# Sketched attention and a SwiGLU block on one core: nine more units with products of parts, and another order of the down products

## The chip, the cores and the metric

The kernel runs on one core of one Trainium2 chip. The metric is the device time in microseconds (us), as the median of several runs. Engines are named as in the profile: PE is TensorE (PEld its weight loads), DVE is VectorE, ACT is ScalarE, POOL is GpSimd, SP issues the DMAs.

## The reference

```python
# attention: batch 4, heads 4, sequence 1088, head_dim 32, sketches of r = 8
def phi(x):
    a = np.einsum('rd,bhsd->bhsr', S1, x)
    b = np.einsum('rd,bhsd->bhsr', S2, x)
    return np.einsum('bhsi,bhsj->bhsij', a, b).reshape(*x.shape[:-1], r * r)
q_p, k_p = (phi(q), phi(k))
kv = np.einsum('bhsf,bhsd->bhfd', k_p, v)
z = np.sum(k_p, axis=2)
num = np.einsum('bhsf,bhfd->bhsd', q_p, kv)
den = np.einsum('bhsf,bhf->bhs', q_p, z)[..., None] + 1e-06
# x: (4 * 1088, 128), the attention's output with the heads side by side
g = x @ w_gate                          # w_gate, w_val: 128 x 1536
silu = g * (1.0 / (1.0 + np.exp(-g)))
val = x @ w_val
return (silu * val @ w_out).astype(np.float32)   # w_out: 1536 x 128
```

The inputs of the SwiGLU block come as 64-bit floats and are narrowed on the chip.

## The kernel before

**Tiling.** The 4352 tokens stand as columns of `xT` (128 x 4352). They are cut into blocks: the first batch's 1088 tokens into blocks 0, 1 and 2 with 384, 384 and 320 columns, the other 3264 into six blocks of 480 and one of 384 (`HEAD` is the first of these, `line` lists them). The 1536 hidden channels are 12 chunks of 128. A *unit* (i, j) is the gate and the value product of block i with chunk j, the Silu on ACT, and on DVE the product of both into a hidden slot. A *down product* (`down`, L1082) multiplies one hidden slot by its chunk of `w_out` and adds it up in the bank of its block.

**Two kinds of units.** A plain unit (`unit`, L1034) is one fp32 matmul for the gate and one for the value; the trace shows two records for each of them. A unit *of parts* splits weight and tokens into a high and a low part and their difference, all in fp32r: `start_unit` issues two matmuls with the differences (L997) and an ACT copy of the two sums (L1000), `finish_unit` adds four more matmuls (L1010, L1011), then the Silu (L1013) and the DVE product (L1018). `cut_weights` (L871) makes the parts of a weight chunk (three chunks of 128 columns at a time) in four steps: ACT high part, a subtraction, ACT low part, a last step for the difference, where the second and fourth are on POOL or DVE. `cut_tokens` (L881, L884, L889) does so for a block's tokens. Before the change, units of the first batch are plain and all units of the `line` are of parts.

**Order.** Everything is emitted in an order written by hand; each engine works through its own queue in that order. The first batch's units after the opening ones follow `seq`, 30 units with index z from 0 to 29: z 12 to 20 are chunks 6 to 8 of blocks 0, 1, 2, and z 21 to 29 are chunks 9 to 11 of blocks 0, 1, 2. The narrowing of the weights (`narrow`, via `part`) is threaded between the first 22 of them. From z = 17 on each unit is followed by one down product and by one step of `attentions()`, the generator that prepares the attention of the next batches: `turn_keys` and `turn_queries` (DVE transposes), key products (L354, PE), four feature products (L377, DVE), `feature_sums` (L547, POOL), key values and value sums (L388, L717, PE), `fold` (L601 to L608, DVE), query sketches (L342, PE) with their copies (L590, ACT), `query_step` (L745 to L762: the denominators and three pairs of a feature product and a transpose into `phT`, all DVE), and `numerators` (L780, PE) with copies into `xT` (L797, ACT and DVE). The step that ends with the numerators yields "first"; block `HEAD` can be cut after it. When `seq` is done, a loop issues the down products that are left, three at a time, each time with a step of the attention. The last two follow `start_unit` of the first unit of the `line`. Then come the 84 units of the `line`.

**Banks.** PSUM has eight banks here. `bank` hands out single ones in turn (`g0`, `g1`, `g2` and up to z = 16 `acc`), `pair` the pair used longest ago of (0,1), (4,5), (6,7) that is not held, `wide("a")` and `wide("b")` are the pairs (4,5) and (6,7). `let_go` ends a hold.

**Rooms.** `room` has ten slots of 384 columns; the six opening units keep their Silu in slots 0 to 5 until `catch_up` (L1058, POOL) multiplies it in. Tiles with one tag share a number of buffers (`bufs`), and a new one waits for the last reader of the oldest.

## Time and profile before

| | |
|---|---|
| median of 3 runs | 278.8 us (278.59 to 278.91) |
| the profiled execution | 278.89 us, span 277.2 us |
| busy: PE, DVE, ACT, POOL | 271.4, 203.7, 184.5, 98.9 us |
| plain gate and value products (L1034) | 28.7 and 28.0 us busy, 72 records each |
| matmuls of units of parts | L997, L1010, L1011: 84 records for each of the six |
| copies of sums (L1000, ACT) | 84, 78.5 us |
| clock granted to TensorE | full |

The span runs from the first to the last instruction; the profiled execution's own time holds 1.7 us around it. Matmuls are pipelined, so a record's duration overlaps the next one: the distance from start to start is what a matmul costs TensorE. In a row of the groups stand the line, the engine, the operation, output and inputs by name, the count, then busy time and mean duration, then the idle time before them and who ended it. In a timeline stand the start, the time covered by the merged instructions, the engine, the line, the names and the count.

### The profile page before, as it was taken

How to read it: one execution, taken by the hardware profiler on the slowest of the kernel's cores; microseconds unless marked ns; L12 is line 12 of the kernel's file. 1: busy time of each engine (PE TensorE's matmuls, PEld its weight loads, DVE VectorE, ACT ScalarE, POOL GpSimd, SP SyncE). 2: the span in 40 equal slices, each digit the busy share in tenths (PEclk: the TensorE clock that was granted, in tenths of full speed). 3: DMA queues.
4: the chain of work that ended last, by engine and by line, in shares of the span. 5: the costliest groups of instructions: out<-in, count | busy, mean ns of one | idle time of the engine just before them, and what ended most of it. 6: DMA issues, size and time to landing. Idle time of an engine off the chain costs nothing.

```text
span 277.2 us, 5670 instructions
## 1 busy us (share of the span) xinstructions
PE 271.4 (98%) x2169; PEld 198.3 (72%) x2169; DVE 203.7 (74%) x355; ACT 184.5 (67%) x330; POOL 98.9 (36%) x110
## 2 busy tenths in 40 slices
PE   8899999999999999999999999999999999999995
PEld 7645565666766787777577777867887888788994
DVE  3997987977688873887545766967877995987431
ACT  3468665565421586667479898769879878886860
POOL 3313422179820440060034353435425553542000
PEclk9999999999999999999999999999999999999999
DMA  6573195221151123000200020000100200010011
GB/s 192 168 220 79 54 277 185 74 89 57 39 114 28 26 85 94 2 1 0 38 13 4 0 39 0 0 2 10 27 0 2 36 0 1 9 29 0 10 29 28
DMA packets 26139, 14.30 MB, mean 52 GB/s; under 512 B 19840, under 2 KB 24192, under 8 KB 26112
## 3 DMA queue, kind: packets, MB, share of 16 engines
q1 hardware_dynamic: 25456, 13.84, 19.4%
q8 instruction: 17, 0.28, 0.4%
q10 hardware_dynamic: 656, 0.10, 0.2%
q14 instruction: 10, 0.08, 0.1%
HBM read 11.41 MB, written 2.23 MB: 49 GB/s over the span
## 4 chain that ended last, share of the span: by engine, by line
PE 94%; DVE 2%; DMA 2%; ACT 1%; issue 0%; SPq 0%
PE PS L1082 22%; PE PS L1034 16%; PE PS L1010 13%; PE PS L997 13%; PE PS L1011 13%; PE PS L1074 2%; PE PS L1077 2%; PE PS L1076 2%; PE PS L354 2%; PE PS L780 2%; PE PS L342 2%; PE PS L388 2%; DMA kld<-in_k_dram 2%; PE PS L1110 1%; PE PS L497 1%; PE PS L445 1%
## 5 line engine op out<-in xcount | busy, mean ns | idle before, releaser
L1000 ACT ACTIVATE PS<-PS 128x960 f32<-128x960 f32 (+1 forms) x84 | 78.5, 935 | 32.0 <-PE PS L997 31.2
L1018 DVE SCALAR_TENSOR_TENSOR hbuf<-PS,sg 128x480 f32<-128x480 f32 (+1 forms) x84 | 53.7, 640 | 43.6 <-ACT sg L1013 40.8
L1013 ACT ACTIVATE sg<-PS 128x480 f32<-128x480 f32 (+1 forms) x84 | 46.7, 556 | 2.0 <-PE PS L1011 1.2
L997 PE MATMUL PS<-xd,gphq 128*128 128x480 f32 (+1 forms) x84 | 47.3, 564 | 0.0
L1082 PE MATMUL PS<-hbuf,wo 128*128 128x480 f32 (+3 forms) x118 | 45.9, 492 | 0.0
L1010 PE MATMUL PS<-x,graw 128*128 128x480 f32 (+1 forms) x84 | 32.1, 382 | 0.0
L1011 PE MATMUL PS<-x,wb 128*128 128x480 f32 (+1 forms) x84 | 31.6, 376 | 0.0
L997 PE MATMUL PS<-xd,wd 128*128 128x480 f32 (+1 forms) x84 | 31.4, 374 | 0.0
L1010 PE MATMUL PS<-x,w 128*128 128x480 f32 (+1 forms) x84 | 31.4, 374 | 0.0
L1011 PE MATMUL PS<-x,graw 128*128 128x480 f32 (+1 forms) x84 | 31.3, 373 | 0.0
L1034 PE MATMUL PS<-xT,wg 128*128 128x384 f32 (+1 forms) x72 | 28.7, 480 | 0.0
L1034 PE MATMUL PS<-xT,wv 128*128 128x384 f32 (+1 forms) x72 | 28.0, 470 | 0.2 <-DVE wv L286 0.2
L1082 PEld LDWEIGHTS PS<-hbuf,wo 128*128 128x128 f32 x118 | 22.1, 189 | 7.4 <-issue 0.9
L1038 ACT ACTIVATE sg<-PS 128x384 f32<-128x384 f32 (+1 forms) x30 | 13.8, 465 | 18.8 <-PE PS L1034 17.2
L997 PEld LDWEIGHTS PS<-xd,gphq 128*128 128x128 f32 x84 | 15.8, 188 | 10.0 <-ACT PS L1000 6.4
L997 PEld LDWEIGHTS PS<-xd,wd 128*128 128x128 f32 x84 | 15.8, 189 | 9.9 <-issue 6.7
L884 POOL TENSOR_TENSOR x<-xT,x 128x480 fp32r<-128x480 f32 (+1 forms) x6 | 7.2, 1195 | 37.6 <-ACT x L881 37.6
L1034 PEld LDWEIGHTS PS<-xT,wv 128*128 128x128 f32 x72 | 13.4, 190 | 8.9 <-DVE hbuf L1049 0.9
L1034 PEld LDWEIGHTS PS<-xT,wg 128*128 128x128 f32 x72 | 12.9, 189 | 9.3 <-issue 1.2
L1010 PEld LDWEIGHTS PS<-x,graw 128*128 128x128 f32 x84 | 15.7, 187 | 3.5 <-ACT PS L1000 0.8
L1082 PE MATMUL PS<-hbuf,scaled 128*128 128x480 f32 x36 | 17.4, 565 | 0.0
L1010 PEld LDWEIGHTS PS<-x,w 128*128 128x128 f32 x84 | 15.8, 188 | 2.2
(184 smaller groups left out, 494.5 us busy)
## 6 DMA issues: line engine op xcount, KB each, us to landing
kld<-in_k_dram SPq DMA_DIRECT2D x4, 544.0 KB, 4.4
vld<-in_v_dram SPq DMA_DIRECT2D x12, 144.0 KB, 4.7
qld<-in_q_dram SPq DMA_DIRECT2D x3, 544.0 KB, 4.2
raw<-in_moe_w_out_dram SPq DMA_DIRECT2D x4, 384.0 KB, 4.0
raw<-in_moe_w_gate_dram SPq DMA_DIRECT2D x3, 384.0 KB, 3.6
raw<-in_moe_w_val_dram SPq DMA_DIRECT2D x3, 384.0 KB, 3.7
out_dram<-o SPq DMA_DIRECT2D x16, 60.0 KB, 2.0
vld<-in_v_dram SPq DMA_DIRECT2D x4, 112.0 KB, 4.3
```

The source lines that it names most:

```text
L342: nc.tensor.matmul(ps[32 * a : 32 * a + 32, 96 * (c - c0) : 96 * (c - c0) + 96], qT[:, 4 * c + a, :], s123[:, a : a + H, :, :].rearrange(" ...
L354: nc.tensor.matmul(ps[32 * a : 32 * a + 64, 64 * (c - c0) : 64 * (c - c0) + 64], kT[:, c, a : a + 2, :].rearrange("p a t -> p (a t)"), s12 ...
L884: engine.tensor_tensor(out=x0[:, 0:n], in0=x, in1=whole(x1[:, 0:n]), op=ALU.subtract)
L997: nc.tensor.matmul(ps[:, k], w_parts[id(w), j // 3][2][:, j % 3, :], xd, start=True, stop=True)
L1000: nc.scalar.activation(ps, ps, AF.Copy, scale=-1.0 / WHOLE)
L1010: nc.tensor.matmul(ps[:, k], w1, x1, start=False, stop=False, skip_group_check=True)
L1011: nc.tensor.matmul(ps[:, k], wb, x0, start=False, stop=True, skip_group_check=True)
L1013: nc.scalar.activation(sg, ps[:, 0], AF.Silu, scale=WHOLE)
L1018: nc.vector.scalar_tensor_tensor(out=hj[:, 0:n], in0=ps[:, 1], scalar=WHOLE, in1=sg, op0=ALU.mult, op1=ALU.mult)
L1034: nc.tensor.matmul(o[:, 0:n], w[:, j, :], xT[:, t0 : t0 + n], start=True, stop=True)
L1038: nc.scalar.activation(sg[:, 0:n], g[:, 0:n], AF.Silu)
L1082: nc.tensor.matmul(acc[i][:, 0:n], w, hidden[i, j][:, 0:n], **sides)
```

## The change

The units z = 21 to 29 become units of parts, started one ahead. For this the parts of the weight chunks must be there earlier: chunk 3 (channels 9 to 11) of both weights is split at z = 11 to 18, in its own rooms (`home`), with DVE for the second and fourth step. The tokens of blocks 0, 1, 2 are split at z = 18, 21, 24. The other three chunks are split later, much as before. The down products come in another order (blocks 0 and 1 with chunks 0 to 8, then chunks 9 to 11 of both, then block 2), and two of them follow units 17, 18, 21, 22 and 23, so that 18 instead of 13 are issued within the list. `catch_up` moves from z = 24 to 26 to z = 18 to 20. In the attention, pairs are taken by `pair`, the sums of features are issued one by one between the feature products, the second key products with their copies come ahead of the value sums, and one more step is taken at z = 25. The `exp` and `man` tiles have 5 and 4 buffers instead of 6 each.

```diff
+    narrow_bufs = dict(exp=5, man=4)
...
-            stage.tile(shape, I32, tag=n + tag, name=n, bufs=6) for n in ("exp", "man")
+            stage.tile(shape, I32, tag=n + tag, name=n, bufs=narrow_bufs[n]) for n in ("exp", "man")
...
-            lambda: add(s[:, 0:2, :], rows[:, 0:2, :], rows[:, 4:6, :]),
-            lambda: add(s[:, 2:4, :], rows[:, 2:4, :], rows[:, 6:8, :]),
-            lambda: add(s[:, 0:2, :], s[:, 0:2, :], s[:, 2:4, :]),
+            lambda: add(s, rows[:, 0:2, :], rows[:, 2:4, :]),
+            lambda: add(s, s, rows[:, 4:6, :]),
+            lambda: add(s, s, rows[:, 6:8, :]),
...
-        hold("a")
-        kp = wide("a")
+        kp = pair("keys")
...
+            if n == 0:
+                zs, sums = feature_sums(phk)
+            else:
+                sums.pop(0)()
             if n == 3:
-                release("a")
+                let_go("keys")
             if n % 3 != 1:
                 yield
-        zs, sums = feature_sums(phk)
-        for f in sums:
-            f()
+        sums.pop(0)()
         yield from turn_keys(2)
-        kvz = wide("a")
+        kvz = pair("values")
         key_values(kvz[:, 0, 0:F], phk, 0, NC)
+        kab, copies = sketched(pair(), key_products, 2, "kab2")
+        run_copies(copies, 2)
         value_sums(kvz[:, 0, :], zs)
-        kab, kcopies = sketched(wide("b"), key_products, 2, "kab2")
         fold(kvz[:, 0, :])
         spread = spread_out(1, kvz[:, 0, :])
-        hold("a", "b")
+        let_go("values")
         yield
-        qab, copies = sketched(wide("a"), query_sketches, 3, "qab")
+        qab, copies = sketched(pair(), query_sketches, 3, "qab")
         run_copies(copies, 2)
         yield
-        run_copies(kcopies, 2)
-        release("a", "b")
...
+    def home(w, c):
+        if w is wg:
+            if c == 3:
+                return [big("phq", k) for k in range(3)]
+            return [big("raw", k) if k < 8 else big("phq", 3) for k in range(3 * c, 3 * c + 3)]
+        if c == 3:
+            t = const.tile([P, 3, 3, P], F32R, name="v3")
+            return [t[:, k] for k in range(3)]
+        return [
+            stage.tile([P, 3, P], F32R, tag=tag, name=name, bufs=narrow_bufs[tag])[:]
+            for tag, name in (("exp", "w1"), ("man", "wb"), (("exp", "man")[c % 2], "wd"))
+        ]
...
-            acc[i] = bank("g1" if i == 1 else "g2" if i in line[2::2] else "acc")
+            acc[i] = bank("g2" if i == 1 or i in line[2::2] else "acc")
...
-    order = [(i, j) for i in range(3) for j in range(NCH)]
+    order = [(i, j) for i in (0, 1) for j in range(9)]
+    order += [(i, j) for i in (0, 1) for j in range(9, NCH)] + [(2, j) for j in range(NCH)]
+    PARTS = 21
...
-        unit(i, j)
+        if z < PARTS:
+            unit(i, j)
+            if z == PARTS - 1:
+                start_unit(*seq[PARTS])
+        else:
+            ahead_first = z != 26
+            for start in (ahead_first, not ahead_first):
+                if not start:
+                    finish_unit(i, j)
+                elif z + 1 < len(seq):
+                    start_unit(*seq[z + 1])
...
-        if z in (24, 25, 26):
+        if z in (18, 19, 20):
             catch_up()
...
-        if z >= 17:
+        for _ in range({17: 2, 18: 2, 21: 2, 22: 2, 23: 2}.get(z, 1) if z >= 17 else 0):
             todo.remove(order[0])
             todo.insert(0, order.pop(0))
             down()
+        if z == 11:
+            gates3 = cut_weights(wg, (3,), [free_room(7)], nc.vector)
+            values3 = cut_weights(wv, (3,), [free_room(6)], nc.vector)
+        for lag, steps in enumerate((gates3, values3) if z >= 11 else ()):
+            if z - lag in (11, 13, 15, 17):
+                take(steps[(z - lag - 11) // 2], 1)
+        if z in (18, 21, 24):
+            run(cut_tokens((z - 18) // 3, soon=True))
...
         if z >= 17:
-            parts_of(1)
+            parts_of(1 + (z == 25))
         if z == 26:
-            take(low, 1)
-            take(third, 3)
+            take(third, 2)
         if z == 29:
-            take(second, 1)
             take(third, 1)
         if z == 23:
-            lows = [room[:, 6 + c, :].rearrange("p (c f) -> p c f", f=P) for c in range(4)]
-            gates = cut_weights(wg, lows, nc.vector)
-        for row, at in enumerate(((23, 24), (25, 26, 27, 28), (27, 28))):
-            if z in at:
-                take(gates[row], 4 // len(at))
-    todo.sort()
+            gates = cut_weights(wg, range(3), [free_room(k) for k in (8, 9, 7)], nc.vector)
+        for row, at in enumerate(((23, 23, 24), (25, 26, 28), (27, 27, 29))):
+            take(gates[row] if z in at else [], at.count(z))
+    todo.sort(key=order.index)
...
-        parts_of(1 + (begun[0] and len(todo) > 2))
+        parts_of(1 + begun[0])
```

`start_unit` and `finish_unit` take the block and the chunk instead of an index into the `line`, and do the same as before.

## The prediction

> **What bounds the kernel now.** I read the page first, then the busy time by stretches, then the timelines of TensorE and VectorE between 47 and 95 us, then the waits of that stretch.
>
> ```profile
> span 277.2 us, 5670 instructions
> ...
> PE 271.4 (98%) x2169; PEld 198.3 (72%) x2169; DVE 203.7 (74%) x355; ACT 184.5 (67%) x330; POOL 98.9 (36%) x110
> ```
>
> TensorE is busy 98% of the span, so all else matters only where it makes TensorE wait. Next the stretches: units 21 to 29 of the list, and the down products after them.
>
> ```profile
> core 0: us, PE busy (x) PEld busy (x) DVE busy (x) ACT busy (x) POOL busy (x), PEclk, DMA share, GB/s
> ...
> 54.80:76.80 22.00, 22.00 (x277) 14.55 (x276) 15.86 (x29) 12.01 (x30) 17.63 (x17) 1.00 0.22 70
> 76.80:92.00 15.20, 15.20 (x111) 9.40 (x110) 13.30 (x22) 2.56 (x6) 1.76 (x1) 1.00 0.31 65
> ```
>
> TensorE has no gap there. In the second stretch VectorE is nearly as full (13.30 of 15.20), and the two timelines show why:
>
> ```profile
> 76.84 4.03 PE L1082 MATMUL PS<-hbuf,wo 128*128 128x384 f32 x12
> 80.71 2.10 PE L1082 MATMUL PS<-late,wo 128*128 128x384 f32 x6
> 82.64 4.25 PE L1082 MATMUL PS<-hbuf,wo 128*128 128x384 f32 x14
> 86.82 1.57 PE L780 MATMUL PS<-phT,spread 32*32 32x288 f32 x64
> 88.32 0.81 PE L1082 MATMUL PS<-hbuf,wo 128*128 128x320 f32 x2
> 88.96 2.86 PE L1082 MATMUL PS<-late,wo 128*128 128x320 f32 x10
> 91.42 0.62 PE L997 MATMUL PS<-xd,gphq 128*128 128x480 f32 x1
> ```
> ```profile
> 76.65 0.42 DVE L745 TENSOR_TENSOR dot<-qab 128x288 f32<-128x288 f32 x1
> ...
> 85.53 0.98 DVE L762 STREAM_TRANSPOSE phT<-phq 128x768 f32<-128x768 f32 x1
> ...
> 90.03 0.65 DVE L889 SCALAR_TENSOR_TENSOR xd<-x,xT 128x480 fp32r<-128x480 f32 x1
> ```
> ```profile
> PEld PS L780 <- DVE phT L762: 0.4, 1, 0.4
> ```
>
> The second batch's numerators (L780) begin when VectorE has its last phT, after a chain of 9.9 us from `dot` (76.65 to 86.5). The down products between are filler that just covers it: the weight load even waited 0.4 us. After the numerators xd is ready at 90.68, but six more down products of 320 columns hold TensorE until 91.8 (in the chain of waits L997 begins at 91.82). So **two things bound this stage, TensorE's work and VectorE's chain, level with each other**. That decides how much of a saving in products can be kept.
>
> **What the skill says.** The page "TensorE: Matmul & The Clock Gate" (section "Wait — 56ns, not 53.3ns?") has a warm matmul start every N / 2.4 GHz + about 2.5 ns, 165 ns for 384 columns; the trace has 175 ns in the last block, near it. The page "FP8 and Floating Point Precision" (section "TensorE Precision Notes") counts four passes for true FP32: the trace has 0.645 us for a plain product of 384, 3.7 times the 175 ns. "SBUF — State Buffer" (section "SBUF: two separate sides") says a VectorE operation with two SBUF inputs and a GpSimd operation that reads SBUF lock each other out: the trace agrees, the L871 subtraction on VectorE takes 0.55 us with GpSimd idle and up to 1.19 beside it. The TensorE page's "Architectural detail" calls ScalarE's and VectorE's queues strict FIFO; so does this trace, each in program order.
>
> **The change, part by part.**
>
> *Products.* Whole plain units with 384 columns are 2 x 0.645 = 1.29 us, with 320 columns 2 x 0.54 = 1.08 (L1034 starts at 75.76, 76.30 and 76.84).
>
> ```profile
> 252.10 0.34 PE L997 MATMUL PS<-xd,wd 128*128 128x384 f32 x1
> 252.27 0.34 PE L1010 MATMUL PS<-x,graw 128*128 128x384 f32 x1
> 252.45 0.34 PE L1011 MATMUL PS<-x,graw 128*128 128x384 f32 x1
> ```
>
> Durations overlap; the starts give the pitch, 0.175 us. A unit of parts is six: 1.05 us. For 320 columns no row exists; from 0.217 us at 480 and 0.175 at 384 I work out an estimate of 0.147, so 0.88. Six units save 0.24, three save 0.20: **2.05 us of TensorE work**. The 36 down products stay; only their order and place change.
>
> *Added on ScalarE:* the copy of the sums (L1000: 0.795 us for 768 columns, some 0.68 for 640 by the same slope), nine times: 6 x 0.80 + 3 x 0.68 = 6.8 us, and three high parts of tokens (L881), about 0.5 each. ScalarE had 12.0 us in 22; four of its weight parts (0.51 each) leave for units 11 to 16, so it comes to about 18 in 21. It fits in sum. What is queued behind each copy is the Silu of the unit before, and behind that the next copy: a late one holds TensorE's `finish_unit`. I find about 0.7 us of this at the last unit, where two weight parts stand ahead of the copy; it falls beside VectorE's chain and costs nothing unless that chain is shorter than I think, then 0.7.
>
> *Added on VectorE and GpSimd:* three xd (0.5 to 0.9 us: 0.65 at 480 columns with GpSimd idle, 0.94 on average), three low parts on GpSimd (1.1 us for 384, L884), and one value chunk's two steps from GpSimd to VectorE. GpSimd's 17.6 us in 22 begin earlier, with the catch-ups at units 18 to 20; its last feature sum is due at about 69.8, by the value sums at 70.7. Zero on the path, at most 0.9 if it is late by one operation.
>
> *Split weights at 11 to 18:* VectorE takes four steps of about 0.55 us more between 42 and 52 us, where it was idle 0.2 to 0.6 us per unit. From the rows, the product L1049 of units 15 and 16 comes about 0.9 us later, in time for the bank that the unit two later needs (48.3 against 48.4). Zero, at most 0.3. The smaller exp and man pools cost nothing: only two fills are under way at once; the third value part waits for wo's fill on GpSimd (about 58.2), with a copy and a Silu ahead of it (else 0.5, beside 1.2 us of key products). The order of feature additions costs the same: four of 128x512 and 128x256 shapes as before, spread out earlier. SP's queue keeps its loads in order, and block 0's store moves into the last stretch, with nobody waiting for it but the transpose counted below. Block 1's sums move from bank g1 to g2, last used by unit 20 and taken at unit 22: free by then, else 0.3.
>
> *Order of the stage.* Unit 17 starts at 47.72 as before. I add up: units 17 to 20 with six down products and the first start take 8.75 us, to 56.5. Units 21 to 23, with two down products each, take 3 x 2.34 + 1.2 for the key products = 8.2, to 64.7. Here the attention holds one of three bank pairs, and unit 25's start waits for VectorE's product of unit 23, behind a weight step and two feature products: 0.4 us, to 65.1. Units 24 and 25 are 1.70 each, with 1.03 + 1.2 + 0.24 for key values, key products and value sums: 70.95. The second key products now stand ahead of the value sums, so the fold (1.85 us from the value sums' end at 69.23 to 71.06 in the trace) ends at 72.8. Unit 26 ends at 72.6; the query sketches start at about **72.85, against 72.31 before**, and end at 74.5. Then one ScalarE copy (0.5), unit 28's copy (0.65), unit 27's Silu (0.4) and VectorE's product (0.45) stand before `dot`: 76.5, against 76.65. Five fewer down products were left, but five more were done ahead of the sketches; that is what eats the saving up to here.
>
> From `dot` VectorE does 2.0 us of denominators, six operations of 0.98, two unit products of 0.45, one weight step of 0.5 and one store transpose of 0.55: 9.85 us, where it took 9.9 before with 0.9 of idle time in it. So phT is complete at about 86.4, the **numerators begin at about 86.7** (before 86.9), and end at 88.3. TensorE gets there at 86.6 by its own work with the 0.7 us stall. Now four down products (2.15 us) stand before `start_unit(HEAD, 0)` where six stood (3.45 from 88.37 to 91.82). xd needs 2.3 us after the numerators (88.37 to 90.68), so L997 starts at about 90.65 against 91.82: **1.1 to 1.2 us gained**. The main line behind is the same in both; its attention steps are reached one unit earlier, before group 4.
>
> Sum against the profiled execution: span 277.2 - 1.1 = 276.1, and 278.89 - 1.1 = 277.8; the profiled run lies 0.1 above the median of 278.8, so I say 277.7.
>
> **The rivals.** *(a) All the work saved shows:* VectorE's chain is 0.8 us or more shorter or starts earlier (the before trace has 0.9 us of idle time in it, waiting for a late Silu), TensorE stays full, and 2.05 us go: 276.75. For it speaks TensorE's full row before; against, that six down products no longer separate numerators and xd. *(b) No change that shows:* the chain starts 0.6 to 1.6 us later, by GpSimd's lock or sums that come late; 278.3 to 279.3. *(c) Slower: bank pairs.* With one pair held for keys or values, each start waits for VectorE's product two units back. I find 0.4 us once; if it comes at each of the six starts from unit 23 to 28, the query sketches slip by 5 x 0.4 = 2.0 us more, and everything behind them: 278.8 - 1.1 + 2.0 = 279.7. It decides from a slip of 1.7 us on. For it: VectorE already had 15.9 of 22 us, and takes more. Against: the doubled down products stand in just those three units. *(d) The edit does not do what it says:* the diff issues f32r products for units 21 to 29; an x part not ready would turn (c) on, nothing else.
>
> **How the numbers follow.** What a measurement of this kernel can tell from no change is about 0.2%, 0.56 us. My case 0.46 (277.1 to 278.2), (a) 0.20, (b) 0.16, (c) with (d) 0.18. So faster 0.66, same 0.16, slower 0.18. The range runs from (a) with a little of the 0.3 us of other waits, 276.5, to 279.5, within (c).
>
> **What would show it.** In the profile after: L1034 falls from 72 to 54 records for each weight and L997 rises by nine each. Query sketches (L342) at 72.5 to 73.2, `dot` at 76.2 to 77, numerators at 86.3 to 87.2 with idle TensorE before them put down to phT, and L997 of the main line at 90.3 to 91. If numerators begin below 86, (a) is right; if units 23 to 28 show TensorE waiting for VectorE's L1018, (c). The prediction is wrong if the sketches move by over 1 us or the stage from 92 us on changes its own length.

## The result, and the profile after

The changed kernel takes **283.07 us** (median of 4 runs, 282.82 to 284.36) against 278.86 for the kernel before on the same chip: ratio 1.0148, 95% interval 1.01 to 1.0197. It is slower by 4.2 us where the forecast was 1.1 us faster and the range ended at 279.5. The profiled execution took 283.04 us, with a span of 281.3.

The page of the changed kernel, span and busy times, and the row of the plain gate products (line, engine, operation, names and shape, count | busy us, mean ns | idle before):

```profile
span 281.3 us, 5734 instructions
...
PE 270.2 (96%) x2187; PEld 200.2 (71%) x2187; DVE 208.9 (74%) x360; ACT 192.3 (68%) x342; POOL 100.7 (36%) x111
...
L1042 PE MATMUL PS<-xT,wg 128*128 128x384 f32 (+1 forms) x54 | 21.4, 479 | 0.0
```

The plain products fell to 54 records, as the diff says. Line numbers move with the edits: the start products of a unit of parts are L997 before, L1006 in the changed kernel and L1015 in the later ones; VectorE's product of such a unit is L1018, L1026 and L1035, a down product L1082, L1090 and L1099 or L1100.

TensorE is busy 1.2 us less than before, and the span is 4.1 us longer: TensorE waits. The busy time by stretches of the changed kernel tells where:

```profile
core 0: us, PE busy (x) PEld busy (x) DVE busy (x) ACT busy (x) POOL busy (x), PEclk, DMA share, GB/s
49.00:58.00 9.00, 8.83 (x33) 5.76 (x31) 9.00 (x17) 4.73 (x11) 4.34 (x4) 1.00 0.11 26
58.00:70.00 12.00, 10.10 (x72) 7.56 (x73) 8.24 (x15) 8.09 (x18) 9.93 (x10) 1.00 0.21 75
70.00:91.40 21.40, 20.00 (x280) 14.04 (x280) 17.64 (x30) 9.23 (x20) 6.42 (x7) 1.00 0.30 73
```

Before, TensorE had no gap in any of these. The first of the three in the kernel before:

```profile
49.00:58.00 9.00, 9.00 (x63) 5.88 (x61) 7.67 (x17) 5.52 (x14) 3.05 (x4) 1.00 0.24 74
```

From 49 to 58 VectorE has no gap left (9.00 of 9.00, where it was 7.67). The timeline of TensorE in the changed kernel names the waits; in brackets stand the idle time before the row and who ended it:

```profile
57.50 0.33 PE L1019 MATMUL PS<-x,v 128*128 128x384 f32 x1
59.90 1.56 PE L1090 MATMUL PS<-late,wo 128*128 128x384 f32 x4 [2.07 <-POOL wo L288]
...
63.75 0.81 PE L1090 MATMUL PS<-late,wo 128*128 128x384 f32 x2
...
66.09 1.46 PE L1090 MATMUL PS<-hbuf,wo 128*128 128x384 f32 x4
...
73.23 0.69 PE L356 MATMUL PS<-s,kT 128*64 128x64 f32 x16 [0.16 <-DVE kT L329]
...
75.94 1.69 PE L344 MATMUL PS<-s,qT 128*32 128x96 f32 x72
...
87.28 2.96 PE L1090 MATMUL PS<-hbuf,wo 128*128 128x320 f32 x10 [1.24 <-DVE o L1132]
90.71 1.57 PE L782 MATMUL PS<-phT,spread 32*32 32x288 f32 x64
...
94.50 0.48 PE L1006 MATMUL PS<-xd,graw 128*128 128x480 f32 x1
...
100.63 0.46 PE L1006 MATMUL PS<-xd,wd 128*128 128x480 f32 x1 [1.47 <-DVE hbuf L1026]
```

**Wait A, 2.07 us** at 57.8: the seventh down product needs chunks 6 to 8 of `w_out`, the third of four pieces that `narrow` makes. **Wait B, 1.24 us** at 86.0: block 2's first down product takes the bank `acc`, and block 0's sums leave it only with the transpose of its store (L1132, VectorE). **Wait C, 1.47 us** at 99.2: the start of the line's fourth unit takes the bank pair of its first, and VectorE makes the first unit's product (L1026), which frees that pair, only at 99.88. The main line begins at 94.50 against 91.42, 3.08 us late; waits A, B and the 0.16 make 3.47, the saving of 2.05 stands against them, and so about 1.7 us (3.08 - 3.47 + 2.05) are lost where the records show no idle time of TensorE; the last experiment shows how such losses look. With wait C that is 4.55 us; about 0.4 come back further down, which I did not follow.

What made these three late stands in the queues of VectorE and GpSimd of the changed kernel:

```profile
52.05 1.13 DVE L265 TENSOR_SCALAR exp<-raw 128x384 int32<-128x384 int32 x1
53.10 1.15 DVE L266 TENSOR_SCALAR man<-raw 128x384 int32<-128x384 int32 x1
...
85.78 0.98 DVE L764 STREAM_TRANSPOSE phT<-phq 128x768 f32<-128x768 f32 x1
86.69 0.54 DVE L1132 STREAM_TRANSPOSE o<-PS 128x384 f32<-128x384 f32 x1
...
94.94 3.85 DVE L379 TENSOR_TENSOR phk<-kab 128x768 f32<-128x768 f32 x4
98.72 0.83 DVE L329 STREAM_TRANSPOSE kT<-kld 128x640 f32<-128x640 f32 x1
...
99.88 0.61 DVE L1026 SCALAR_TENSOR_TENSOR hbuf<-PS,sg 128x480 f32<-128x480 f32 x1
```
```profile
51.96 1.00 POOL L894 TENSOR_TENSOR x<-xT,x 128x384 fp32r<-128x384 f32 x1
52.91 1.12 POOL L1066 TENSOR_TENSOR hbuf<-hbuf,room 128x384 f32<-128x384 f32 x1
...
58.86 0.99 POOL L288 TENSOR_TENSOR wo<-man,exp 128x384 f32<-128x384 f32 x1 [4.82 <-DVE man L279]
...
96.66 1.58 POOL L549 TENSOR_TENSOR zs<-phk 128x512 f32<-128x512 f32 x1 [20.16 <-DVE phk L379]
```

The rows of the kernel before to hold against them:

```profile
51.41 0.35 DVE L263 TENSOR_SCALAR exp<-raw 128x384 int32<-128x384 int32 x1
51.68 0.35 DVE L264 TENSOR_SCALAR man<-raw 128x384 int32<-128x384 int32 x1
...
55.95 1.00 POOL L286 TENSOR_TENSOR wo<-man,exp 128x384 f32<-128x384 f32 x1 [5.38 <-DVE man L277]
...
61.38 0.81 PE L1082 MATMUL PS<-late,wo 128*128 128x384 f32 x2
...
91.17 2.76 DVE L377 TENSOR_TENSOR phk<-kab 128x768 f32<-128x768 f32 x4
```

For A: two narrowing steps (L265, L266) took 1.13 and 1.15 us beside GpSimd's catch-ups and first token parts; they took 0.35 each before, with GpSimd idle. Three further steps that the change adds stand ahead of the same piece in VectorE's queue: the last steps of chunk 3's two weights, one of them lengthened to 1.10 us beside GpSimd, and the first xd. So the piece of `w_out` was whole at 59.85, against 56.95 before, 2.9 us later. At the same time it is asked for 3.6 us earlier, because two down products follow units 17 and 18: at about 57.8, where before it was 61.38. Before, 4.43 us lay between the two (61.38 - 56.95). By this subtraction either shift alone would have fitted in; both together leave the wait of 2.07. For C: the four feature products (L379) took 3.85 us beside GpSimd's sums, 2.76 before, and one more attention step puts the `kT` transpose ahead of the first unit's product (L1026).

### The profile page after: what moved, and what is told of

It is laid out like the page before. It is cut to its first block, busy times and chain, and to the rows that moved or that the text cites. A ratio compares the mean times of both kernels' runs of the same rounds, so it can differ in the third digit from the quotient of the medians.

```text
span 281.3 us, 5734 instructions
## 1 busy us (share of the span) xinstructions
PE 270.2 (96%) x2187; PEld 200.2 (71%) x2187; DVE 208.9 (74%) x360; ACT 192.3 (68%) x342; POOL 100.7 (36%) x111
## 4 chain that ended last, share of the span: by engine, by line
PE 79%; DVE 12%; issue 3%; DMA 2%; ACT 1%; SPq 1%; POOL 0%; DVEq 0%; ACTq 0%
PE PS L1090 17%; PE PS L1018 13%; PE PS L1006 13%; PE PS L1019 13%; PE PS L1042 8%; PE PS L1085 2%; PE PS L1082 2%; PE PS L1084 2%; PE PS L782 2%; PE PS L356 2%; DMA kld<-in_k_dram 2%; DVE late L1057 1%; DVE kT L329 1%; PE PS L390 1%; PE PS L344 1%
## 5 line engine op out<-in xcount | busy, mean ns | idle before, releaser
L1009 ACT ACTIVATE PS<-PS 128x960 f32<-128x960 f32 (+2 forms) x93 | 85.4, 919 | 34.7 <-PE PS L1006 33.9
L1026 DVE SCALAR_TENSOR_TENSOR hbuf<-PS,sg 128x480 f32<-128x480 f32 (+1 forms) x90 | 56.9, 632 | 44.4 <-ACT sg L1021 41.6
L1021 ACT ACTIVATE sg<-PS 128x480 f32<-128x480 f32 (+2 forms) x93 | 50.9, 548 | 2.8 <-PE PS L1019 2.1
L1090 PE MATMUL PS<-hbuf,wo 128*128 128x480 f32 (+3 forms) x118 | 45.8, 493 | 1.2 <-DVE o L1132 1.2
L1006 PE MATMUL PS<-xd,gphq 128*128 128x480 f32 (+2 forms) x51 | 29.5, 579 | 0.0
L1090 PEld LDWEIGHTS PS<-hbuf,wo 128*128 128x128 f32 x118 | 22.0, 190 | 7.7 <-DVE o L1132 1.9
L1006 PE MATMUL PS<-xd,wd 128*128 128x480 f32 (+1 forms) x63 | 23.6, 375 | 1.5 <-DVE hbuf L1026 1.5
L894 POOL TENSOR_TENSOR x<-xT,x 128x480 fp32r<-128x480 f32 (+2 forms) x9 | 10.5, 1168 | 38.8 <-ACT x L891 38.7
L1018 PE MATMUL PS<-x,graw 128*128 128x480 f32 (+1 forms) x63 | 23.9, 380 | 0.0
L1019 PE MATMUL PS<-x,wb 128*128 128x480 f32 (+1 forms) x63 | 23.6, 374 | 0.0
L1019 PE MATMUL PS<-x,graw 128*128 128x480 f32 (+1 forms) x63 | 23.5, 374 | 0.0
L1018 PE MATMUL PS<-x,w 128*128 128x480 f32 (+1 forms) x63 | 23.5, 373 | 0.0
L1006 PE MATMUL PS<-xd,graw 128*128 128x480 f32 (+1 forms) x42 | 22.6, 537 | 0.0
L1006 PEld LDWEIGHTS PS<-xd,wd 128*128 128x128 f32 x63 | 11.9, 189 | 9.2 <-issue 4.2
L1090 PE MATMUL PS<-hbuf,scaled 128*128 128x480 f32 x36 | 17.4, 565 | 0.0
L986 POOL TENSOR_TENSOR hlate<-hbuf,hlate 128x480 fp32r<-128x480 f32 x10 | 13.0, 1305 | 9.8 <-ACT hlate L985 7.7
L1006 PEld LDWEIGHTS PS<-xd,gphq 128*128 128x128 f32 x51 | 9.6, 189 | 6.3 <-ACT PS L1009 2.8
```

The source lines that it names most:

```text
L894: engine.tensor_tensor(out=x0[:, 0:n], in0=x, in1=whole(x1[:, 0:n]), op=ALU.subtract)
L986: add_to(before, y + 2, lambda: nc.gpsimd.tensor_tensor(out=h0, in0=h, in1=whole(h1), op=ALU.subtract))
L1006: nc.tensor.matmul(ps[:, k], w_parts[id(w), j // 3][2][:, j % 3, :], xd, start=True, stop=True)
L1009: nc.scalar.activation(ps, ps, AF.Copy, scale=-1.0 / WHOLE)
L1018: nc.tensor.matmul(ps[:, k], w1, x1, start=False, stop=False, skip_group_check=True)
L1019: nc.tensor.matmul(ps[:, k], wb, x0, start=False, stop=True, skip_group_check=True)
```

## The experiments

Theory: the nine cheaper units save what was reckoned, and three waits of an order written by hand (A, B, C), with VectorE lengthened by GpSimd, give back more. Rivals: the units of parts themselves wait for ScalarE or for a bank pair; or VectorE is simply full, and a wait that is removed returns at another place. The ratio is always to the kernel before, on the same chip.

### Each wait by itself

**Down products in an order that asks for the late piece later** (against wait A):

```diff
-    order = [(i, j) for i in (0, 1) for j in range(9)]
+    order = [(0, j) for j in range(6)] + [(1, j) for j in (0, 1, 3, 4, 5, 2)]
+    order += [(i, j) for i in (0, 1) for j in range(6, 9)]
```

> The changed kernel with another order of the down products alone: chunks 0 to 5 of block 0, then chunks 0 to 5 of block 1, then chunks 6 to 8 of both; counts per unit stay. No down product now needs the third chunk group of w_out before unit 24. Theory 1 (the 2.07 us that TensorE stood still at 57.7 us for POOL's last narrowing step is a wait of its own): it goes, nothing takes its place, and the time falls by 1.8 to 2.2 us, to about 281.0. Rival (VectorE's late queue sets the stage, as the prediction had it; the down product only shows it first): units 21 to 23 wait for VectorE's products instead, and the time falls by less than 0.7 us.

282.45 us, ratio 1.0121 [1.0095, 1.0147]: only 0.6 us, as the rival had it. In TensorE's timeline of this run wait A is gone, B and C stand, and two others have come:

```profile
66.26 0.44 PE L1006 MATMUL PS<-xd,v 128*128 128x384 f32 x1 [1.12 <-DVE hbuf L1026]
72.84 0.32 PE L719 MATMUL PS<-zs,ones 128*32 128x64 f32 x8 [0.77 <-POOL zs L549]
```

The first is the prediction's rival (c): the start of unit 25 has no bank pair until VectorE has made the product of unit 23. The second is the feature sums, late on GpSimd. Of 2.07 us removed, 1.12 + 0.77 = 1.89 reappear: what is late for A is late for the next thing too. Why 0.6 us were won and not 0.2 I did not follow.

**Block 0's down products complete early** (against wait B):

```diff
+    order = [(0, j) for j in range(9)] + [(1, j) for j in range(3)] + [(0, j) for j in range(9, NCH)]
```

> The changed kernel with another order of the down products alone: after unit 23's, the last three of block 0 come at once, so that block 0 is stored while the list still runs and its bank is free long before block 2's first product. Theory 1 (the 1.24 us before 87.28 us is a wait for the bank, which VectorE frees late because the store's transpose stands behind a step of the feature chain): it goes and the time falls by 1.0 to 1.4 us, to about 281.9. Rival (VectorE's chain to the numerators is the bound): the wait moves to the numerators and the time stays within 0.4 us.

281.67 us, ratio 1.0112 [1.0069, 1.0154]: 1.4 us less than the changed kernel. Wait B is gone, and A and C stand as they were (2.07 and 1.48). So B was the order alone, and its removal is kept in full.

**One attention step less in the pass ahead of the main line** (against wait C):

```diff
-        parts_of(1 + begun[0])
+        parts_of(1 + (begun[0] and len(todo) > 2))
```

> The changed kernel with the number of attention steps in the last turns as before the change, so that the step with the feature sums and the key transpose comes after the first unit of the main line and not ahead of it. Theory 1 (the 1.47 us at 99.2 us come from that step standing ahead of VectorE's first product): the wait falls to 0.6 us or less and the time by 0.8 to 1.5 us, to about 281.9. Rival (the four feature products themselves, slowed to 3.85 us by POOL's sums beside them, are what delays it): less than 0.5 us.

283.81 us, ratio 1.0161 [1.0131, 1.0191]. Wait C fell from 1.47 to 0.73 us, and the features still took 3.85; the median doesn't show a gain. The stretches and one row of TensorE's timeline of this run say why it is even higher:

```profile
core 0: us, PE busy (x) PEld busy (x) DVE busy (x) ACT busy (x) POOL busy (x), PEclk, DMA share, GB/s
55.00:60.00 5.00, 2.92 (x13) 2.00 (x12) 4.70 (x11) 4.57 (x10) 1.29 (x2) 0.97 0.35 115
60.00:65.00 5.00, 5.00 (x46) 3.25 (x47) 2.03 (x3) 1.23 (x4) 4.81 (x5) 0.69 0.34 111
```
```profile
59.76 2.93 PE L1090 MATMUL PS<-late,wo 128*128 128x384 f32 x4 [2.08 <-POOL wo L288]
```

After wait A TensorE's granted clock (the column PEclk) fell to 0.69 over 5 us, and the four matmuls took 2.93 us instead of 1.56. Three of this kernel's four runs had a mean granted clock of 0.993 or 0.994; the fourth, at the full clock, took 282.82, no less than the fastest of the changed kernel. So by itself this edit shows the shorter wait, but no time.

**All three together** (the first order, with block 0's chunks 9 to 11 put in ahead of block 1's chunks 6 to 8, and one attention step less):

```diff
+    order = [(0, j) for j in range(6)] + [(1, j) for j in (0, 1, 3, 4, 5, 2)] + [(0, j) for j in range(6, NCH)]
```

> All three edits together (chunks 0 to 5 of blocks 0 and 1, then chunks 6 to 11 of block 0 and the rest; the attention steps as before the change). If the three waits are independent, 2.07 + 1.24 + 1.0 to 1.47 us go: 278.3 to 278.8, level with the kernel before, and the 2.05 us of saved products are then still spent on some 1.5 us of small waits. If they cover one another or VectorE's chain becomes the bound: 279.5 to 281.

280.33 us, ratio 1.0054 [1.0033, 1.0074], 2.7 us less than the changed kernel. The orders against A and B gave 0.6 and 1.4 by themselves; if these add, 0.7 is left for the third part, which is what its wait lost. That they add was not tried in pairs. Four waits are left: 1.12 for L1026 at unit 25, 0.76 for `zs`, 0.18 for phT and 0.72 in the line.

### The lock between VectorE and GpSimd

**Catch-ups at units 3 to 5 instead of 18 to 20,** in the changed kernel:

```diff
-        if z in (18, 19, 20):
+        if z in (3, 4, 5):
```

> The changed kernel with the three catch-ups of POOL moved from units 18 to 20 to units 3 to 5, where POOL is mostly idle; nothing else. In the changed kernel's trace two VectorE steps of the third w_out narrowing take 1.13 and 1.15 us beside POOL instead of 0.35 each. Theory 1 (VectorE and POOL locking each other out between 50 and 61 us is what makes the narrowing late): these two steps shorten by at least 0.8 us in all, the wait of 2.07 us for POOL's last narrowing step falls to 0.3 to 1.2 us, and the time by 0.9 to 1.8 us, to some 281.5. Rival (the added split steps and the order of VectorE's queue make it late, whatever POOL does): the wait stays above 1.7 us and the time within 0.4 us of the changed kernel.

283.05 us, ratio 1.0139 [1.0106, 1.0173]. Wait A fell from 2.07 to 1.27 (the trace is of an execution of 283.66 us, 0.6 above the median), and nothing was won. So 0.8 us of wait A come from the catch-ups; the rest stays with the steps added on VectorE and GpSimd's token part, beside which L265 still takes 1.12. The waits of TensorE's weight loads from 26 to 49 us in this run:

```profile
PEld PS L1042 <- DVE hbuf L1057: 2.6, 7, 0.6
```

In the changed kernel the same row has 0.9 us in 3 waits. At their earlier place the catch-ups lengthen the narrowing steps there (L279 to 1.35 us), units 3 to 16 wait for VectorE's products, and unit 17's first down product starts at 50.30 instead of 49.01. **The price of the lock moved with the operation.** The same move on top of all three repairs:

> All three edits (the down order that avoids the late w_out chunks and stores block 0 early, and one attention step less ahead of the main line) together with the catch-ups at units 3 to 5. Theory 1 (with the down order mended, the lateness of VectorE and POOL showed as 1.12 us before unit 25's start and 0.77 us before the value sums): both fall to 0.5 us or less and the time goes from 280.3 to between 278.6 and 279.3. Rival (VectorE's own work bounds units 21 to 26): above 279.8.

280.98 us, ratio 1.0077 [1.0053, 1.0101]: 0.65 more than without it. The wait for `zs` is gone, the one at unit 25 is 1.24 instead of 1.12, and unit 17's down product is 0.87 us later (49.70 for 48.83).

**The order of the feature sums put back** for the later batches, on top of that: with the changed order GpSimd can add after the second feature product, with the former one after the third.

```diff
+                lambda: add(t[:, 0:2, :], rows[:, 0:2, :], rows[:, 4:6, :]),
+                lambda: add(t[:, 2:4, :], rows[:, 2:4, :], rows[:, 6:8, :]),
+                lambda: add(t[:, 0:2, :], t[:, 0:2, :], t[:, 2:4, :]),
...
-                zs, sums = feature_sums(phk)
+                zs, sums = feature_sums(phk, True)
```

> The kernel of the run before in this list, with the feature sums of the later batches added in the old order again (rows 0 and 1 with 4 and 5 first), so that POOL can't start them before VectorE's third feature product. Theory 1 (the four feature products at the head of the main line took 3.85 us instead of 2.76 for POOL's early start beside them): they fall below 3.2 us, the 0.7 us wait at the third unit goes, and the time falls by 0.5 to 0.9 us. Rival (the lock only moves to the next operations): less than 0.3 us.

280.08 us, ratio 1.0039 [1.0029, 1.0049], 0.9 less. VectorE's timeline of this run:

```profile
93.30 2.75 DVE L379 TENSOR_TENSOR phk<-kab 128x768 f32<-128x768 f32 x4
```

The features are back at the time that they had before the change, and no wait is left in the line. So of wait C one part was the step, and the other the sums that begin beside the features: here both the wait and the time went.

**The fourth piece of `w_out` narrowed wholly on VectorE,** at the end of unit 23, with the late sums and the three repairs, the catch-ups at units 18 to 20 and block 2's low parts of tokens behind the sums:

```diff
-            engine = nc.vector if split else nc.gpsimd
+            engine = nc.vector if split or (name, i) == ("wo", 3) else nc.gpsimd
...
+        if z == 23:
+            part("wo", 3)
```

> From the kernel with all three edits (280.3 us; catch-ups at units 18 to 20 as in the change) with the old order of the later batches' sums, and two further moves that take VectorE and POOL work out of units 22 to 25: the last step of the fourth w_out narrowing goes to the end of unit 23, wholly on VectorE, where VectorE stood idle for 1.17 us, and the low part of block 2's tokens goes to POOL after the feature sums. Theory 1 (VectorE's and POOL's queues, not TensorE's or ScalarE's, make the two waits before unit 25's start, 1.12 us, and before the value sums, 0.77 us): both fall to 0.4 us or less, the sums' order gives another 0.6 to 0.9, and the time is 277.5 to 278.4, under the kernel before. Rival (ScalarE's nine copies and Silus are the bound once these are gone): waits for L1009 or the Silu take their place, 279 or more.

281.28 us, ratio 1.0083 [1.0056, 1.011] (279.41 in the one run at the full clock, where 277.5 to 278.4 was expected). The rival, ScalarE, is not what TensorE waited for either. VectorE's three steps now ran beside GpSimd's sums, in its timeline:

```profile
65.83 1.17 DVE L273 SCALAR_TENSOR_TENSOR exp<-raw,exp 128x384 int32<-128x384 int32 x1
66.92 1.65 DVE L279 SCALAR_TENSOR_TENSOR man<-raw,man 128x384 f32<-128x384 uint32 x1
68.60 1.53 DVE L288 TENSOR_TENSOR wo<-man,exp 128x384 f32<-128x384 f32 x1
```

4.35 us, against 0.54 each for the first two beside an idle GpSimd. The `kT` transpose behind them was awaited for 1.94 us.

**The same with the catch-ups at unit 26,** behind the sums, and block 1's chunks 0 to 2, which need them, behind block 0's last:

> The kernel of the run before in this list with the catch-ups at unit 26, when POOL has its sums done, and the first three products of block 1 behind its others (their bank is opened by chunk 3 in place of chunk 0). Theory 1 (catch-ups at units 18 to 20 cost VectorE by the lock on SBUF): VectorE's first two steps of the third w_out narrowing fall from 2.3 us together to 1.5 or less, and the time falls by 0.2 to 0.8 us against the run before. Rival (with the down order mended, that lateness is covered): the same within 0.2 us.

281.68 us, ratio 1.013 [1.0091, 1.0169]; the two runs at the full clock took 281.2 and 281.3, 1.8 more than that of the run before. The two steps of wait A went from 2.28 to 1.47 us, but the fourth piece came late:

```profile
70.21 0.91 PE L1100 MATMUL PS<-hbuf,wo 128*128 128x384 f32 x2 [3.51 <-DVE wo L288]
```

Block 0's chunk 9 now comes before block 1's first chunks, and so asks for the fourth piece earlier: the fault of wait A once more.

### Towards a version without waits

The last kernels keep the late sums and the shorter step, with the fourth piece of `w_out` in its old place. Block 1's chunks 0 to 2 are added last, so that the catch-ups can come at unit 27, and block 2's low parts of tokens stand behind the sums (the edit against the kernel with the late sums):

```diff
+    order = [(0, j) for j in range(6)] + [(1, j) for j in (3, 4, 5)] + [(0, j) for j in range(6, NCH)]
+    order += [(1, j) for j in (6, 7, 8, 0, 1, 2)]
...
-        if z in (3, 4, 5):
-            catch_up()
+        if z == 27:
+            for _ in range(3):
+                catch_up()
```

> From the kernel with all three edits (280.3 us): old order of the later batches' sums, catch-ups at unit 27 with their three down products behind the others of block 1, and block 2's low part on POOL after the feature sums; the fourth w_out narrowing stays at units 19, 20 and 22 on POOL, as in the change. So POOL has three operations less up to unit 26, and no operation is added anywhere. Theory 1 (POOL's queue and the lock with VectorE make the waits in units 21 to 26): VectorE's steps of the fourth narrowing take less than the 0.90 and 1.36 us they took with all three edits, the wait before unit 25's start falls from 1.12 to 0.8 us or less, the one before the value sums from 0.77 to 0.3 or less, and the time is 278.0 to 278.9. Rival (VectorE's number of operations is the bound, and the lock only shifts waiting time): waits of 1.5 us or more remain, 279.3 or more.

279.54 us, ratio 1.0018 [0.9981, 1.0056], above the 278.0 to 278.9 of the theory. One long wait stays, the bank pair for unit 25, 1.24 us. VectorE's product stood behind narrowing steps beside the values' low parts on GpSimd, so these go behind the sums as well (`take(low, 3)` and `take(second, 3)` from units 21 and 25 to one place at unit 25):

> The same, with the three low parts of the value weights also moved on POOL from unit 21 to behind the feature sums at unit 25 (and ScalarE's steps that need them behind them), so that POOL has little beside VectorE's fourth narrowing and feature products. Theory 1: the narrowing's two steps return to some 0.55 us each, the wait before unit 25's start falls to 0.3 us or less, and the time is 277.4 to 278.3, under the kernel before. Rival: the low parts, now beside the fold and the key copies, hold ScalarE's copy of unit 27 and TensorE with it, 278.6 or more.

279.18 us, ratio 1.0011 [1.0001, 1.0022]. That wait is gone, and the prediction's own bound appears, the numerators behind VectorE's chain (the trace is of an execution of 279.74 us, 0.6 above the median):

```profile
88.98 1.56 PE L791 MATMUL PS<-phT,spread 32*32 32x288 f32 x64 [1.22 <-DVE phT L773]
```

Two explanations were tried for that wait: that too many down products ahead of the sketches begin the chain late (one instead of two behind units 17 and 18), or that the catch-ups beside the chain lengthen it (moved to unit 19).

```diff
-        for _ in range({17: 2, 18: 2, 21: 2, 22: 2, 23: 2}.get(z, 1) if z >= 17 else 0):
+        for _ in range({21: 2, 22: 2, 23: 2}.get(z, 1) if z >= 17 else 0):
```

> The last kernel (279.2 us, where the three long waits are gone and TensorE waits 1.22 us for VectorE's last transpose ahead of the numerators) with one down product instead of two behind units 17 and 18, so that two more are left for the stretch between the query sketches and the numerators. Theory A (the change puts too many down products ahead of the query sketches, and VectorE's chain that starts from them then ends late): the sketches start 1.1 to 1.3 us earlier, the wait for the last transpose falls below 0.3 us and the time falls by 0.9 to 1.3 us, to about 278.1. Theory B (VectorE needs the time that the doubled products give it at units 17 to 20): waits of VectorE's products return at units 21 to 23, and the time changes by less than 0.4 us.

278.75 us, ratio 0.9998 [0.9988, 1.0009]: 0.4 less, though the intervals of the two ratios overlap. The sketches begin at 72.56 instead of 74.44; the wait is still 1.06 and not below 0.3, since block 0's store transpose now stands in the chain.

> The same kernel of 279.2 us with the three catch-ups on POOL at unit 19, behind block 0's low part, instead of unit 27, where they stood beside VectorE's denominators and first feature product (0.71 + 0.79 + 1.35 us, against 0.45 + 0.46 + 0.95 without POOL). Theory C (the lock with these catch-ups is what lengthens the chain): the chain from its first product to the last transpose falls from 10.7 us to 9.6 or less and the time by 0.7 to 1.2 us. Theory B as above: VectorE's steps at 53 to 58 us grow instead and a wait of over 0.7 us comes at units 21 to 23.

279.86 us, ratio 1.0035 [1.0012, 1.0058]. The chain is shorter (9.75 us instead of 10.7) and the wait 0.27, but at unit 19 the catch-ups lengthen the token steps of unit 21 instead:

```profile
56.73 0.44 PE L1015 MATMUL PS<-xd,gphq 128*128 128x384 f32 x1 [1.22 <-DVE xd L908]
```

Both together:

> Both edits of the last two kernels. If A and C hold and are independent, VectorE's chain ends before TensorE has done its down products: TensorE's work is the bound and the time is 277.2 to 277.9, under the kernel before (278.8). If VectorE lacks the time at units 17 to 20 (B), 278.5 to 279.5, and the kernel before isn't beaten this way.

280.82 us, ratio 1.0076 [1.0054, 1.0098]: the wait for xd grows to 1.87, since two down products fewer stand ahead of it; the mean granted clock of the profiled run was 0.992, and the two runs at the full clock took 280.2 and 280.4.

Last, two steps are taken out of the chain: block 0 is completed earlier, so that its store transpose comes at unit 26, and the third low part of the gate's weights goes behind the chain (the edit against the kernel with two down products back).

```diff
+    order = [(0, j) for j in range(6)] + [(1, 3)] + [(0, j) for j in range(6, NCH)]
+    order += [(1, j) for j in (4, 5, 6, 7, 8, 0, 1, 2)]
...
-        for row, at in enumerate(((23, 23, 24), (25, 26, 28), (27, 27, 29))):
+        for row, at in enumerate(((23, 23, 24), (25, 26), (27, 27))):
```

> The version with two of the down products put back, and two things taken out of VectorE's chain between dot and phT: block 0's down products with chunks 6 to 11 come directly behind block 0's and one of block 1's first, so that the transpose of block 0's store (0.57 us) stands at unit 26, ahead of the chain; and the third low parts of the gate's weights (0.52 us) come with the last steps of the main line's opening, behind the chain. Theory (VectorE's chain sets the numerators): phT is complete 0.9 to 1.1 us earlier, the wait of the numerators falls from 1.06 us to 0.2 or less, and the time comes to 277.6 to 278.2, under the kernel before (278.7). Rival (TensorE and locks elsewhere set it): the wait goes, but comes back as another (the store's transpose holds up a unit's product, or w_out's seventh chunk is awaited again); 278.5 or more.

278.67 us, ratio 1.0001 [0.999, 1.0013]: level with the kernel before, and with the kernel it was made from (0.9998), where the theory had 277.6 to 278.2. The wait before the numerators halved, to 0.52, and no time was won by it:

```profile
86.79 1.56 PE L791 MATMUL PS<-phT,spread 32*32 32x288 f32 x64 [0.52 <-DVE phT L773]
...
91.37 0.62 PE L1015 MATMUL PS<-xd,graw 128*128 128x480 f32 x1
```

This kernel issues 2.05 us less of TensorE work up to there and has no wait over 0.52, yet its main line begins at 91.37 against 91.42. Its stretches and a piece of its timeline show how:

```profile
49.00:58.00 9.00, 9.00 (x36) 5.84 (x34) 9.00 (x19) 6.08 (x13) 2.39 (x3) 1.00 0.18 64
58.00:70.00 12.00, 11.85 (x165) 9.07 (x164) 10.32 (x16) 8.14 (x19) 8.48 (x9) 1.00 0.14 48
70.00:91.40 21.40, 20.86 (x227) 14.47 (x227) 19.27 (x31) 9.13 (x20) 10.13 (x10) 1.00 0.34 77
```
```profile
62.86 1.45 PE L1100 MATMUL PS<-late,wo 128*128 128x384 f32 x4
63.85 0.63 PE L1015 MATMUL PS<-xd,gphq 128*128 128x384 f32 x1
64.47 0.45 PE L1015 MATMUL PS<-xd,v 128*128 128x384 f32 x1
64.76 0.34 PE L1027 MATMUL PS<-x,gphq 128*128 128x384 f32 x1
```

Four down records begun at 62.86 are worth 4 x 0.3225 = 1.29, and one start product 0.175: the second start product could begin at 64.33, and begins at 64.47. The next follows after 0.29 instead of 0.175. That is 0.25 us lost in this unit without a single row of idle time, since records of pipelined matmuls cover the gap. Here it is VectorE that holds it up: its product of unit 23, which frees the bank for the second start product, ends at 64.42. Added up so against the kernel before: 0.6 in units 21 to 23, 0.5 in key values and key products (whose 36 matmuls come in two parts), 0.6 at the numerators, 0.2 before unit 17, about 0.1 elsewhere, 2.0 in all. VectorE is busy 38.6 of these 42.4 us, 34.0 before: **the change takes 2 us from TensorE and puts 4.6 on VectorE**.

Most of these 4.6 us are operations made longer, not operations added. Beside GpSimd two of the three xd took 1.40 and 1.48 us here, where one beside an idle GpSimd takes 0.55; the last step of a weight took 1.11 for 0.55, a narrowing step 0.51 for 0.35, and the denominators with the first feature product 1.2 more than without the catch-ups beside them. That is an estimate of 3.7 us; like lengthenings that both kernels have cancel.

Is it VectorE, then, that sets the pace? The waits of TensorE's weight loads from 40 to 92 us name it, but not it alone (L1018 is in this kernel ScalarE's copy of a unit's sums):

```profile
PEld PS L1015 <- DVE hbuf L1035: 0.9, 2, 0.5
PEld PS L1027 <- ACT PS L1018: 0.6, 2, 0.4
PEld PS L390 <- ACT PS L1018: 0.5, 1, 0.5
```

VectorE in turn waited 1.6 us in this stretch for ScalarE's Silu. So that VectorE sets the pace is read from sums and waits; no kernel with VectorE's work cut away was run, and the copies of sums that the new units add on ScalarE remain a rival that no run separates.

## Why the prediction was wrong, step by step

The span was forecast to fall by 1.1 us and rose by 4.1. Waits A, B and C, 4.78 us together, are most of these 5.2; each stands on a term that the prediction had put at nothing or nearly nothing. The measured time is outside all its rivals too, of which the slowest, (c), was priced at 279.7. Both signs that it named for being wrong came: the sketches moved by 3.6 us (72.31 to 75.94), and the stretch from the main line to the end grew by 1.0 us (185.8 to 186.8).

- *Products, 2.05 us:* held as a count of work: unit 22 with its two down products takes 66.09 - 63.75 = 2.34 us, the figure of the sum. Unit 23, by the same rows, takes 2.58 (to 68.67), with no row of idle time in it. The sum took every unit at its pitch and has no term for such losses, about 1.7 us in the changed kernel.
- *Split weights, "zero, at most 0.3":* **failed, and with it the largest term.** It was asked only what these steps do to the banks of units 15 and 16. Nothing of the kind happens there (unit 17 starts at 47.72 in both). But VectorE's queue came out full, and the narrowing of `w_out` stands in it. The sum then put units 17 to 20 with *six* down products at 56.5 and never asked when the seventh's weights are there. It had the fill on GpSimd at "about 58.2", for another reader; it ended at 59.85, and the seventh product is due at 57.8. Measured 2.07 us of wait. The run that takes this wait away won 0.6 us, so VectorE's lateness behind it counts for more than the one piece.
- *The lock as a price of VectorE's two-input steps only:* failed. The prediction's place in the Trainium skill, "SBUF — State Buffer" (section "SBUF: two separate sides"), names beside them VectorE operations in a two-port mode. The narrowing steps with one input (L265, L266) behave like that sort: 0.35 us alone, 1.13 and 1.15 beside GpSimd. The catch-ups' move to units 18 to 20 was priced only for GpSimd's own sums (at most 0.9), not for what it does to VectorE.
- *Block 0's store, "nobody waiting for it but the transpose":* failed. Block 2's first down product waits for its bank. Measured 1.24, and 1.4 us of time in the run that undoes it.
- *Order of feature additions "costs the same", main line "the same in both":* failed. The additions cost the same, but begin beside the features: 3.85 us for 2.76, and with one more step in the queue 1.47 of wait. The two reversals brought 0.7, if the three repairs add, and 0.9.
- *Start of unit 25, 0.4, and rival (c):* in the changed kernel it is among the small waits; once A is removed it is 1.12 to 1.24, once. Wait C is of its kind, a start that waits for VectorE's product to free its bank, but it comes in the main line, where the prediction saw none. So rival (c) was right that the kernel gets slower, but by luck: A and B are other mechanisms, and its own row of six waits did not come.
- *Sketches 72.85:* 75.94, late by A and the small waits. *Chain from dot to phT, 9.85:* 9.4 (79.63 to 89.0), held. *From the numerators to the line, 86.7 to 90.65:* 3.95 forecast, 3.79 measured, held.
- *ScalarE:* 7.8 us more busy (192.3 - 184.5) for the 8.3 reckoned; no long wait for it, as forecast.

What the sum lacked was not a price but two questions: for each thing that is asked for earlier, when is it ready in the queue that makes it; and for each operation moved onto GpSimd's or VectorE's free time, which operation of the other stands beside it there.

## What to carry to other kernels

Moving a consumer forward is a change for its producer too: look up in the trace of before when each of its inputs is complete, and subtract. Where VectorE and GpSimd share a stage, place their operations as a pair, since a step of 0.35 us can take 1.1 and moving it moves the price with it. Work saved on one engine is not yet time won: here 2 us of products saved were worth nothing even when no wait over 0.52 us was left, while the engine level with TensorE was busy for 4.6 us more.

## What the hardware showed that was not expected

A standstill of TensorE of about 2 us was in some executions followed by a lower granted clock. In the trace of the third experiment it is 0.69 over the 5 us after a standstill of 2.08. The three executions of that kernel with a mean granted clock of 0.993 or 0.994 took 283.8 to 283.9 us, the one with the full clock 282.82, so the wait cost them half as much again as its length. Six of these kernels have a standstill of 1.87 to 3.51 us in this stage; of their 25 executions 13 had a mean granted clock of 0.994 or less. In the ten other variants it was 3 of 113, and in the kernel before 2 of more than 100. A standstill of this length thus makes the lower clock likely, but does not decide it: after the longest, 3.51 us, the profiled execution kept the full clock (1.00 from 66 to 75 us).

The Trainium skill, "TensorE: Matmul & The Clock Gate" (section "Part 1: The HAM clock gate (the "warmup" mystery)"), puts the fall to half speed after an idle window of about 3.4 us and calls its window free-running. Here standstills of 1.87 to 2.08 us were often enough, and one of 3.51 was not always. Whether it depends on where the standstill falls in such a window, no run here shows.
